# Score matmuls of batches 2 to 7 in two slots instead of four, and where their masks and v copies run

## Chip, cores and metric

One core of a Trainium2 chip. The metric is the device time of one execution in microseconds; the kernel before is quoted by the median of its runs.

## The reference

Two stages in a row. Attention over q, k, v of shape (8 batches, 8 heads, 576 positions, 64): the first four heads look at the last 32 positions (local mask), the other four at earlier positions with the same remainder by 32 (strided mask).

```python
mask_local = (rel >= 0) & (rel < stride)
mask_strided = (rel >= 0) & (pos[None, :] % stride == pos[:, None] % stride)
...
attn = exp(scores - max) ; attn /= sum
attn_out = attn @ v
```

Its output, as 4608 tokens of 512 features, goes through a two-layer network with w_in (512 x 2048), Mish and w_out (2048 x 512):

```python
h = x @ w_in
sp = np.where(h > 20.0, h, np.log1p(np.exp(np.minimum(h, 20.0))))
g = h * np.tanh(sp)
return (g @ w_out).astype(np.float32)
```

## The kernel before, in words

The network runs in nine blocks of 512 tokens, `t` = 0 to 8. Both its layers (`mlp1`, `mlp2_seven`) are built from seven products of half size with sums in front and behind, on TensorE (PE), VectorE (DVE) and ScalarE (ACT). The order of every engine's instructions is the order of the program; there is no scheduler.

The attention of batch `t + 1` is woven into the second layer of block `t`: `attn_steps` returns a list `at`, and after step `i` of the second layer the functions in `at[i]` are issued. A step is eight matmuls of `pso`; two steps are one product. This document calls block `t` the one with this `t`; blocks 1 to 6 hold batches 2 to 7 and follow the list that is changed here. Batch 1, in block 0, has another list that the diff leaves alone.

One batch's scores are in parts. Strided: `("s", 0)` and `("s", 1)` with 6 units of 72 columns, `("s", 2)` with 4. Local: `("l", 0)` and `("l", 1)` with 5 units of 96 columns, `("l", 2)` with 2. Each unit is two matmuls, one for each head of a pair, on the upper and lower 64 rows of the array (L310, tile `ps`). Steps:

- `Q` (`qk`, L294): score matmuls into an accumulator, then Exp on ACT (L318) into `P_s` or `P_l`.
- `M` and `G` (`mask`, L320, operation at L324): multiply by the 0/1 mask, on DVE (`M`) or on GpSimd (POOL, `G`).
- `V2` (`pv2`, L357): eight matmuls with v (L340, tile `po`), then reciprocal and normalization on DVE (L365, L366) into `x_s` or `x_l`.
- `X` (`xt`, L371): transposes of the result on PE (`trx`), copied to `xT` by ACT.

PSUM has eight banks: `acc0` and `acc1` of two banks each, two single banks `bank0`, `bank1` for the products of the second layer, and two single slots given out in turn by `tile_t` (`pt`). In the attention steps `x` is `acc0` and `y` is `acc1`. An accumulator can be written again when its last reader is done: `V2("s", 2, y)` waits until the normalization of `V2("s", 0, y)` has read `acc1`.

Around that, in the loop from L914: SP issues loads of local q, k, v and the transposes by DMA (`transpose_by_dma`, L205) that make `kTs`, `qTs`, `kTl`, `qTl`. POOL issues loads of strided q, k, v (`load_qk_str`, `load_early_v_str`), casts local v (`cast_v_loc`, two casts of 128x768) and local q and k, multiplies the local masks, and copies strided v from `vsr` to `vs` (`spread_v_str`). Ahead of the cast of local v POOL makes a small copy from `P_s[1]` to `held` (L943), whose only use is its wait: the cast does not begin before that strided mask is done.

Within the second layer each product ends in work for ACT or DVE: copies of `za` and `zc` out of PSUM, additions at L668, and sums of `gT` into `Sg` (L599), which later products read.

Of the kernel before, what the change touches and what calls it, by code (L numbers as in the profile page):

```python
# [12 lines left out]
AF = mybir.ActivationFunctionType  # L13
# [30 lines left out]
def kernel(ctx, tc, q, k, v, moe_w_in, moe_w_out, out):  # L44
    nc = tc.nc
# [61 lines left out]
    def acc(i, name):  # L107

        pool = ps_z[0] if i == 2 else ps_a
        return pool.tile([128, 2, 512], F32, tag=f"acc{i}", name=name)  # L110
# [10 lines left out]
    def tile_t(name):  # L121
        return ps_t.tile([128, 512], F32, tag="pt", name=name)
# [33 lines left out]
    def spread_v_str(b, eng):  # L156
        cast(eng, vs[b % 2][0:PN, :, :, 0:D], vs_raw().rearrange("p h (j d) -> p h j d", d=D))
# [119 lines left out]
    class Attn:  # L277
# [16 lines left out]
        def qk(self, parts, i_acc, ps=None):  # L294

            biased = ps is not None
            ps, o = ps if biased else acc(i_acc, "ps"), 0
            todo = []
            for kind, i in parts:
                w = WQ if kind == "l" else PN  # L300
                o0 = o
                for x, y in PARTS[kind][i]:
                    for e in range(2):
                        r = slice(64 * e, 64 * e + 64)
                        if kind == "l":
                            lhsT, rhs = kTl[r, y, WQ * x:WQ * x + 128], qTl[r, y, WQ * x:WQ * x + WQ]
                        else:
                            c0 = SU * (4 * y + x)
                            lhsT, rhs = kTs[r, c0:c0 + 128], qTs[r, c0:c0 + PN]
                        nc.tensor.matmul(  # L310
                            ps[:, e, o:o + w], lhsT=lhsT, rhs=rhs, start=not biased, stop=True,
                            skip_group_check=biased,
                        )
                    o += w
                todo.append((kind, i, o0, o - o0))
            for kind, i, o0, nw in todo:
                n, pt = (128, P_l[i]) if kind == "l" else (PN, P_s[i])
                nc.scalar.activation(pt[0:n, :, 0:nw], ps[0:n, :, o0:o0 + nw], AF.Exp, scale=scale)  # L318

        def mask(self, kind, i, meng):  # L320
# [77 lines left out]
    def attn_steps(b, x, y):  # L398

        a = Attn(b)  # L400
        Q = lambda i_acc, *parts: (lambda: a.qk(parts, i_acc))
        M = lambda kd, i: (lambda: a.mask(kd, i, nc.vector))
        V = lambda kd, i: (lambda: a.pv(kd, i))
        X = lambda kd, hf: (lambda: a.xt(kd, hf))
        s0, s1, sl2, l0, l1 = ("s", 0), ("s", 1), (("s", 2), ("l", 2)), ("l", 0), ("l", 1)
        if x == y:
            T = [(lambda n=n, eng=eng: t_step(b, *T_ORDER[n], eng)) for n, eng in enumerate(
                (None, None, None, None, None, nc.scalar, None, nc.scalar))]
            return [
                T[2:4], [Q(x, s0)],  # L410
                [M(*s0), Q(x, s1)],
                [lambda: spread_v_str(b, nc.vector), V("s", 0)],
                [V("s", 1), M(*s1), Q(x, ("s", 2))],
                [V("s", 2), T[4]],
                [V("s", 3), M("s", 2), T[5]],
                [V("s", 4), T[6]],
                [V("s", 5), T[7]],
                [V("s", 6), Q(x, l0)],
                [V("s", 7), M(*l0), Q(x, l1)],
                [X("s", 0), V("l", 0), M(*l1), Q(x, ("l", 2))],  # L420
                [X("s", 1), V("l", 1), M("l", 2)],
                [V("l", 2), V("l", 3)],
                [V("l", 4), V("l", 5)],
                [lambda hf=hf: a.xt("l", hf, nc.vector) for hf in range(2)],
            ], T[0:2]
        V2 = lambda kd, i, z: (lambda: a.pv2(kd, i, z))
        G = lambda kd, i: (lambda: a.mask(kd, i, nc.gpsimd))
        l2 = ("l", 2)
        at = [
            [],  # L430
            [Q(x, s0), Q(y, s1), M(*s0), M(*s1)],
            [],
            [V2("s", 0, y), Q(x, *sl2), M("s", 2)],
            [],
            [V2("s", 2, y), Q(x, l0), G(*l0)],
            [],
            [V2("s", 4, y), Q(x, l1), G(*l1), G(*l2), lambda: nc.scalar.preload_act_table(AF.Mish)],
            [],
            [V2("s", 6, y)],
            [V2("l", 0, x)],  # L440
            [X("s", 0), V2("l", 2, y), X("s", 1)],
            [V2("l", 4, x), X("l", 0)],
            [X("l", 1)],
        ]
        return at
# [10 lines left out]
    def mlp1(t, accs):  # L456
# [65 lines left out]
        def begin():  # L522
            z[1], z[3] = acc(accs[1], "psu"), acc(accs[0], "psu")
            z[2] = [bank(n, "psb")[:] for n in range(2)]
            z[5] = o_pool.tile([128, 2, DM], F32, tag="osb", name="p5")
            product(both(z[1]), 0, a11, b11, first=True)
            for n in range(2):
                nc.scalar.copy(z[2][n], z[1][:, n, :])
            sums_x(t, "2")
            product(both(z[3]), 0, s1, t1, first=True)  # L530
            sums_x(t, "3")
            if t == 1:
                sums_w_in()[3]()
            nc.scalar.copy(z[5][:], z[3][:])
            y[1] = tile_t("psv")[:]
            product([y[1]], 512, a11, b11, first=True)
# [265 lines left out]
    with tc.manual_schedule():  # L802
# [111 lines left out]
        for t in range(NBLK):  # L914
            if t == 0:
                x, y, z = accs
                at, ts = attn_steps(1, y, y)
                at[3] += [lambda: load_early_v_str(2), cast_v1]
                at[12].append(load_rest2)
                at[1].append(lambda: sums_w()[0](lo))  # L920
                at[7].append(lambda: sums_w()[0](hi))
                at[9].append(lambda: sums_w()[1](lo))
                at[11].append(lambda: sums_w()[1](hi))
                at[14].append(lambda: sums_x(1, "1"))
                at[15] += [
                    lambda: spread_v_str(2, Dv),
                ]
                out_accs = (z, x)
            else:
                if t == 1:  # L930
                    split_third()
                x, y = 0, 1
                gT, z, g1 = mlp1(t, (y, x) if t == 1 else (x, y))
                at = attn_steps(t + 1, x, y) if t + 1 < B else []
                if t == 1:
                    at[0].append(lambda: sums_w()[3](hi))
                if t + 2 < B:
                    at[10] += [lambda: transpose_by_dma(t + 2), lambda: load_v_loc(t + 2)]
                    if t + 3 < B:
                        at[10].append(lambda: load_early_v_str(t + 3))  # L940
                if t + 1 < B:
                    at[1] += [
                        lambda: Po.tensor_copy(held[:], P_s[1][0:1, 0, 0:4]),  # L943
                        lambda: cast_v_loc(t + 1, Po),
                    ]
                if t == 1:
                    at[1] += [lambda: load_qk_str(3), lambda: load_early_v_str(3)]
                if t < B - 3:
                    at[7 if t == 1 else 1].append(lambda: load_qk_str(t + 3))
                if t + 1 < B:  # L950
                    at[12].append(lambda: sums_x(t + 1, "1"))
            for i, g in enumerate(g1):
                g()
                if t == 0:
                    for s in ts if i == len(g1) - 1 else ():
                        s()
                    continue
            if t == 0:
                steps = mlp2(t, gT, out_accs, fc_major=True)
            elif t == NBLK - 1:  # L960
                mlp2_last(t, gT, z[5])
                break
            else:
                za, zc = [bank(i, "pso")[:].rearrange("p (n o) -> p n o", n=2) for i in range(2)]
                steps = mlp2_seven(t, gT, z[5], za, zc)
                if t + 1 == B:
                    steps[12] = lambda f=steps[12]: (sums_x(t + 1, "1"), f())
            for i, g in enumerate(steps):
                g()
                if i < len(at):  # L970
                    for s in at[i]:
                        s()
                if t > 0 and i == 9 and t + 2 < B:
                    cast_qk_loc(t + 2, Po, Po)
                    spread_v_str(t + 2, Po)
            if 0 < t < B - 3:
                load_qk_loc(t + 3)

# [29 lines left out]
```

## Time and profile before

| what | us |
|---|---|
| median of 3 runs | 291.82 (291.79 to 292.35) |
| the profiled execution's own time | 291.2 |
| its span | 289.4 |
| blocks 1 to 6, start to start (chain) | 29.7 each |
| PE busy in the span | 283.8 (98%) |
| DVE, ACT, POOL busy | 196.9, 192.8, 109.2 |

The profile is one execution. A row of the timeline gives the start from the span's begin, the length, the engine, the line, the operation and its tiles; rows of like instructions are merged and end in their number. What stands in square brackets is idle time of that engine before the row, and what ended it. Matmul ends are modelled, starts are recorded. The granted TensorE clock is 1.00 throughout.

### The profile page before, as it was taken

The numbers are of one execution on the slowest core, as the hardware profiler recorded it, in microseconds if no ns is written. First come the engines' busy times: TensorE is split into PE (matmuls) and PEld (weight loads), VectorE is DVE, ScalarE is ACT, GpSimd is POOL, SyncE is SP. The second block draws the span as 40 slices with busy tenths as digits, with TensorE's granted clock in tenths as the row PEclk, the third lists the DMA queues.
The fourth block names the chain that finished last, engine by engine and source line by source line (L and its number), as shares of the span: only waits on it lengthen the run. The fifth ranks groups of instructions, "written<-read, shape, count | busy, mean of one in ns | idle before, by whom it ended". The sixth has DMA issues, their size and how long they took to land.

```text
span 289.4 us, 7507 instructions
## 1 busy us (share of the span) xinstructions
PE 283.8 (98%) x3161; PEld 221.2 (76%) x3161; DVE 196.9 (68%) x398; ACT 192.8 (67%) x274; POOL 109.2 (38%) x122
## 2 busy tenths in 40 slices
PE   8999999999999999999999999999999999999994
PEld 3564455686898689868988888788977897788684
DVE  2273167899786777687777777777777767734742
ACT  1578643699657974898579757985799568507820
POOL 8375502140696059404960397027701710000000
PEclk9999999999999999999999999999999999999999
DMA  8999999999999999999999999999590030003004
GB/s 153 186 208 191 192 194 197 183 141 184 223 169 125 191 294 162 150 150 275 172 116 164 275 163 144 172 271 148 83 254 2 2 145 2 0 3 146 2 0 147
DMA packets 103742, 43.29 MB, mean 150 GB/s; under 512 B 86172, under 2 KB 99212, under 8 KB 103708
## 3 DMA queue, kind: packets, MB, share of 16 engines
q1 hardware_dynamic: 86620, 30.05, 61.8%
q0 software_dynamic: 16800, 12.51, 29.7%
q8 instruction: 25, 0.41, 0.6%
q10 hardware_dynamic: 288, 0.25, 0.3%
q14 instruction: 9, 0.07, 0.1%
HBM read 38.38 MB, written 9.44 MB: 165 GB/s over the span
## 4 chain that ended last, share of the span: by engine, by line
PE 95%; DVE 2%; ACT 2%; issue 0%; ACTq 0%
PE pso L691 30%; PE psu L503 10%; PE psh L472 10%; PE psv L503 8%; PE psb L503 7%; PE psb L472 5%; PE po L340 4%; PE pso L750 4%; PE ps L310 4%; PE pso L723 4%; PE un L264 3%; PE trx L379 2%; PE trx L389 1%; ACT Pl L318 1%; PE tr L236 1%; PE tr L250 1%
## 5 line engine op out<-in xcount | busy, mean ns | idle before, releaser
L691 PEld LDWEIGHTS <-gT 128*128 128x128 bf16 x448 | 41.8, 98 | 6.2
L503 PEld LDWEIGHTS <-w_in 128*128 128x128 bf16 x384 | 37.1, 98 | 8.4
L691 PE MATMUL pso<-w_out,gT 128*128 128x256 bf16 x336 | 41.0, 273 | 0.0
L691 PEld LDWEIGHTS <-Sg 128*128 128x128 bf16 x336 | 31.4, 98 | 4.7
L943 POOL COPY held<-Ps 1x4 bf16<-1x4 bf16 x6 | 3.5, 580 | 79.3 <-DVE Ps L324 79.3
L472 PEld LDWEIGHTS <-w_in 128*128 128x128 bf16 x208 | 20.2, 98 | 16.6 <-issue 0.5
L187 ACT COPY xT<-trx 128x576 bf16<-128x576 bf16 x30 | 18.4, 643 | 18.8 <-PE trx L389 13.3
L324 POOL TENSOR_TENSOR Pl<-Pl,consts_sb 128x960 bf16<-128x960 bf16 (+1 forms) x18 | 29.2, 1639 | 4.1 <-ACT Pl L318 3.5
L503 PEld LDWEIGHTS <-Sw 128*128 128x128 bf16 x288 | 28.2, 98 | 3.3
L472 PE MATMUL psh<-xT,w_in 128*128 128x512 bf16 (+1 forms) x136 | 29.4, 366 | 0.1
L691 PE MATMUL pso<-Tw,Sg 128*128 128x256 bf16 x224 | 26.7, 273 | 0.0
L318 ACT ACTIVATE Pl<-ps 128x960 bf16<-128x960 f32 (+1 forms) x24 | 19.3, 808 | 10.8 <-PE ps L310 10.8
L187 ACT COPY osb<-pso 128x512 f32<-128x512 f32 (+1 forms) x17 | 9.3, 549 | 21.9 <-PE pso L691 12.7
L512 ACT ACTIVATE gT<-psu 128x1024 bf16<-128x1024 f32 x16 | 16.4, 1024 | 8.4 <-PE psu L503 8.3
L318 ACT ACTIVATE Ps<-ps 72x864 bf16<-72x864 f32 (+1 forms) x24 | 18.6, 804 | 4.6 <-PE ps L310 4.6
L366 DVE TENSOR_TENSOR x_s<-po,rden 72x512 bf16<-72x512 f32 x28 | 19.2, 687 | 1.0
L599 DVE TENSOR_TENSOR psu<-psb,p 128x512 f32<-128x512 f32 x16 | 11.2, 698 | 11.8 <-PE psb L503 11.0
L483 ACT ACTIVATE gT<-psh 128x1024 bf16<-128x1024 f32 x16 | 16.2, 1024 | 4.3 <-PE psh L472 4.0
L324 DVE TENSOR_TENSOR Ps<-Ps,consts_sb 72x864 bf16<-72x864 bf16 (+1 forms) x21 | 15.1, 721 | 5.2 <-ACT Ps L318 5.2
L599 DVE TENSOR_TENSOR Sg<-gT 128x256 bf16<-128x256 bf16 (+2 forms) x32 | 12.8, 421 | 7.5 <-ACT gT L512 5.9
L503 PE MATMUL psu<-xT,w_in 128*128 128x256 bf16 x128 | 17.9, 272 | 0.0
L503 PE MATMUL psb<-Sx,w_in 128*128 128x256 bf16 x128 | 17.2, 272 | 0.0
(132 smaller groups left out, 607.0 us busy)
## 6 DMA issues: line engine op xcount, KB each, us to landing
vl<-in_v_dram SPq DMA_DIRECT2D x7, 768.0 KB, 6.3
out_dram<-osb SPq DMA_DIRECT2D x9, 512.0 KB, 5.3
out_dram<-p SPq DMA_DIRECT2D x7, 512.0 KB, 6.5
kl<-in_k_dram SPq DMA_DIRECT2D x6, 576.0 KB, 9.8
ql<-in_q_dram SPq DMA_DIRECT2D x6, 576.0 KB, 11.7
qs<-in_q_dram POOLq DMA_DIRECT2D x8, 288.0 KB, 10.7
vsr<-in_v_dram POOLq DMA_DIRECT2D x8, 288.0 KB, 8.0
w_in<-in_moe_w_in_dram POOLq DMA_DIRECT2D x4, 512.0 KB, 9.7
```

Source lines behind the costliest of these rows:

```text
L187: nc.scalar.copy(out_, in_)
L310: nc.tensor.matmul(ps[:, e, o:o + w], lhsT=lhsT, rhs=rhs, start=not biased, stop=True, skip_group_check=biased,)
L318: nc.scalar.activation(pt[0:n, :, 0:nw], ps[0:n, :, o0:o0 + nw], AF.Exp, scale=scale)
L324: meng.tensor_tensor(out=pm, in0=pm, in1=mk[0:n, :].unsqueeze(1).unsqueeze(1).to_broadcast([n, 2, nu, w]), op=ALU.mult,)
L340: nc.tensor.matmul(po[:, h, :], lhsT=pt[0:n, c0:c0 + 128], rhs=rhs, start=True, stop=True,)
L366: nc.vector.tensor_tensor(out=dst.rearrange("p e (h d) -> p e h d", h=4), in0=po[0:m, :, :, 0:D], in1=rden[0:m].unsqueeze(3).to_broadcast( ...
L472: nc.tensor.matmul(ps_u[:, o:o + n], lhsT=w_in[:, cc, fc * 128:(fc + 1) * 128], rhs=xT[:, cc, a:a + n], start=(cc == 2 and (o == 0 or len( ...
L483: nc.scalar.activation(to, tiles[g][:], AF.Mish)
L503: nc.tensor.matmul(p[:, 256 * j:256 * j + 256], lhsT=lhs[:, cc, f:f + 128], rhs=rhs[:, cc], start=(first and j == 0 and cc == 0), stop=(la ...
L512: nc.scalar.activation(gT[:, c:c + src.shape[1], 256 * half_t:256 * half_t + 256], src, AF.Mish,)
L599: nc.vector.tensor_tensor(out=out_, in0=in0, in1=in1, op=op)
L691: nc.tensor.matmul(ps[:, pair, :], lhsT=lhs(c, 128 * pair), rhs=rhs(c), start=(first and pair == 0 and c == 0), stop=(last and c == 7), sk ...
```

## The change

Four edits:

- In `attn_steps`, the third strided part and the third local part are scored at step 1 behind the first two strided parts, and the second local part at step 5 behind the first. The parts that come along write into the two single `pt` slots (`i_acc == "t"`), one for each head of the pair, so that each has two Exps, one for each slot, instead of one.
- The masks follow: `M("s", 2)` on DVE moves to step 1, `G(l2)` to step 3 and so ahead of the two other masks on POOL, `G(l1)` to step 5.
- `held` is copied from `P_s[2]` instead of `P_s[1]`: POOL's cast of local v comes behind the third strided mask.
- Strided v of batches 4 to 7 is spread by ACT at step 7 of blocks 2 to 5; that of batch 3 by DVE at the beginning of block 2, where the load of batch 4's follows. POOL spreads none of them any more.

```diff
         def qk(self, parts, i_acc, ps=None):
             biased = ps is not None
-            ps, o = ps if biased else acc(i_acc, "ps"), 0
+            o = 0
+            if i_acc == "t":
+                ps = None
+                by_e = [tile_t("ps") for _ in range(2)]
+            else:
+                ps = ps if biased else acc(i_acc, "ps")
+                by_e = [ps[:, e, :] for e in range(2)]
...
                         nc.tensor.matmul(
-                            ps[:, e, o:o + w], lhsT=lhsT, rhs=rhs, start=not biased, stop=True,
+                            by_e[e][:, o:o + w], lhsT=lhsT, rhs=rhs, start=not biased, stop=True,
...
                 n, pt = (128, P_l[i]) if kind == "l" else (PN, P_s[i])
+                if ps is None:
+                    for e in range(2):
+                        nc.scalar.activation(
+                            pt[0:n, e, 0:nw], by_e[e][0:n, o0:o0 + nw], AF.Exp, scale=scale
+                        )
+                    continue
...
         at = [
             [],
-            [Q(x, s0), Q(y, s1), M(*s0), M(*s1)],
+            [Q(x, s0), Q(y, s1), Q("t", *sl2), M(*s0), M(*s1), M("s", 2)],
             [],
-            [V2("s", 0, y), Q(x, *sl2), M("s", 2)],
+            [V2("s", 0, y), G(*l2)],
             [],
-            [V2("s", 2, y), Q(x, l0), G(*l0)],
+            [V2("s", 2, y), Q(x, l0), Q("t", l1), G(*l0), G(*l1)],
             [],
-            [V2("s", 4, y), Q(x, l1), G(*l1), G(*l2), lambda: nc.scalar.preload_act_table(AF.Mish)],
+            [V2("s", 4, y), lambda: nc.scalar.preload_act_table(AF.Mish)],
...
             sums_x(t, "3")
             if t == 1:
                 sums_w_in()[3]()
+            if t == 2:
+                spread_v_str(3, nc.vector)
+                load_early_v_str(4)
...
-                    if t + 3 < B:
+                    if t > 1 and t + 3 < B:
                         at[10].append(lambda: load_early_v_str(t + 3))
                 if t + 1 < B:
                     at[1] += [
-                        lambda: Po.tensor_copy(held[:], P_s[1][0:1, 0, 0:4]),
+                        lambda: Po.tensor_copy(held[:], P_s[2][0:1, 0, 0:4]),
                         lambda: cast_v_loc(t + 1, Po),
                     ]
...
+                if 1 < t < B - 2:
+                    at[7].append(lambda: spread_v_str(t + 2, Sc))
...
                     cast_qk_loc(t + 2, Po, Po)
-                    spread_v_str(t + 2, Po)
```

## The prediction

> **What bounds the kernel now.** I read the page first: busy shares, then the chain that ended last.
>
> ```profile
> PE 283.8 (98%) x3161; PEld 221.2 (76%) x3161; DVE 196.9 (68%) x398; ACT 192.8 (67%) x274; POOL 109.2 (38%) x122
> ...
> PE 95%; DVE 2%; ACT 2%; issue 0%; ACTq 0%
> ```
>
> TensorE (PE) is the chain, and in the list of waits it has two in all, 1.2 and 0.2 us, both in the first 17 us. So taking a wait away gains nothing; only less PE time does, and any new PE wait is paid in full. Next the timeline of block 5 (batch 6's attention between the products). Columns: start, us, engine, line, operation.
>
> ```profile
> 190.82 0.56 PE L310 MATMUL ps<-qTs,kTs 64*128 64x72 bf16 x24
> 191.32 1.92 PE L691 MATMUL pso<-Tw,Sg 128*128 128x256 bf16 x16
> 193.07 0.41 PE L340 MATMUL po<-vs,Ps 72*128 72x65 bf16 x8
> 193.41 0.30 PE L310 MATMUL ps<-qTs,kTs 64*128 64x72 bf16 x8
> 193.55 0.25 PE L310 MATMUL ps<-qTl,kTl 64*128 64x96 bf16 x4
> 193.74 1.92 PE L691 MATMUL pso<-Tw,Sg 128*128 128x256 bf16 x16
> 195.49 0.41 PE L340 MATMUL po<-vs,Ps 72*128 72x65 bf16 x8
> 195.83 0.39 PE L310 MATMUL ps<-qTl,kTl 64*128 64x96 bf16 x10
> 196.15 1.92 PE L691 MATMUL pso<-w_out,Sg 128*128 128x256 bf16 x16
> ...
> 200.32 0.41 PE L340 MATMUL po<-vs,Ps 72*128 72x65 bf16 x8
> 200.57 1.04 PE L691 MATMUL pso<-w_out,gT 128*128 128x256 bf16 x8
> ```
>
> Ends are modelled, so I use starts. Scores run as 64*128, all else on the full height. Eight po matmuls followed by a product take 0.25 us (200.32 to 200.57); followed by scores, 0.34 (193.07 to 193.41, 195.49 to 195.83): going into scores costs 0.09. Coming out: 24 narrow score matmuls take 0.50 us, the 8+4 take 0.33, the ten wide 0.32. With a time in proportion to columns this solves to 0.016 us for 72 columns plus a fixed 0.10 to 0.12. So a visit to scores costs about 0.19 us over its matmuls. This is PE time inside "busy", and each batch pays it four times.
>
> Then the engines that feed it in the same stretch, and GpSimd (POOL) in block 1, which is the same sequence 118.75 us earlier (first mask at 73.40 against 192.15).
>
> ```profile
> 191.23 1.66 ACT L318 ACTIVATE Ps<-ps 72x864 bf16<-72x864 f32 x2 [0.15 <-PE ps L310]
> ...
> 192.93 0.60 DVE L324 TENSOR_TENSOR Ps<-Ps,consts_sb 72x864 bf16<-72x864 bf16 x1 [0.18 <-ACT Ps L318]
> 193.46 0.68 DVE L599 TENSOR_TENSOR Sg<-gT,Sg 128x1024 bf16<-128x1024 bf16 x1
> 194.06 0.20 DVE L365 RECIPROCAL rden<-po 72x8 f32<-72x8 f32 x1
> 194.29 0.69 DVE L366 TENSOR_TENSOR x_s<-po,rden 72x512 bf16<-72x512 f32 x1
> 194.90 1.13 DVE L324 TENSOR_TENSOR Ps<-Ps,consts_sb 72x576 bf16<-72x576 bf16 x1
> ```
>
> ```profile
> 74.85 0.58 POOL L943 COPY held<-Ps 1x4 bf16<-1x4 bf16 x1 [12.44 <-DVE Ps L324]
> ...
> 79.36 4.84 POOL L324 TENSOR_TENSOR Pl<-Pl,consts_sb 128x960 bf16<-128x960 bf16 x3
> ...
> 84.09 0.43 PE L340 MATMUL po<-vl,Pl 128*128 128x65 bf16 x8
> ```
>
> The normalization of the first strided pair ends at 194.98 and frees acc1; PE wants it at 195.49, 0.51 spare. POOL starts only when the second strided mask is done, and its second wide mask ends at 83.33 (two of 2.01 us, starts 1.97 apart), 0.76 before PE reads it at 84.09.
>
> **Scores in two slots.** In blocks 1 to 6 the third strided part and local part 2 join the first visit; local part 1 joins local part 0. Four visits become two: 2 x 0.19 = 0.38 us, six times, 2.3 us. The matmuls themselves only move (0.22 us each lot). The two one-bank slots are free: their last readers, Mish of psv, end at 187.65, 3 us before. This is certain; what follows is what eats it.
>
> **The third mask goes ahead on VectorE (DVE).** It waits for its two half Exps. Exp of 864 columns takes 0.88 us, of 576 0.65: by that slope 0.41 for 288; starts lie 0.78 and 0.55 apart, so 0.31 for 288. The first Exp stays at 191.23, so the halves start at 192.80 and 193.11, end at 193.52. The mask starts 0.04 later as its neighbours do, 193.56, and takes 0.45 (445 ns is the shortest of its kind, in batch 1 where POOL is quiet): 194.00. The Sg subtraction behind it starts 0.08 before that end, 193.92, where it started at 193.46. From there to the end of the normalization the rows show 1.52 us: 195.44. PE starts 0.06 after such an end (15.49+0.69 to 16.24, its one such wait): 195.50. PE itself has saved one visit by then, 195.49-0.19 = 195.30. So it waits 0.20 us for acc1, in each of six blocks: 1.2 us. The second visit's saving, 0.19, comes behind that point and stays. Bounds: 0.05 to 0.35, from a mask that ends 0.15 earlier or later.
>
> [...]
>
> **POOL's masks.** The held copy now waits for the third mask: 194.00 against 193.53, so POOL's whole row is 0.47 later, and the small local mask (902 ns, 0.86 to the next start) goes first. Block 1, which has three DMA issues of 0.7 us in front: wide masks from 79.36+0.47+0.86 = 80.69, ending at 82.69 and 84.66. PE's first local pair, at 82.70 before, would come at 82.51 and waits to 82.75 (0.24); the next, due at 84.09-0.19+0.24 = 84.14, waits to 84.72 (0.58). Sum 0.82. Blocks 2 to 4 have two DMA issues: in block 3 the masks began at 137.95, so the second wide one ends at 143.25; due at 143.44-0.19 = 143.25, PE waits about 0.05. Blocks 5 and 6 have none: the mask ends near 201.3, wanted at 202.64, nothing.
>
> **The port.** The two casts of local v start 0.53 us after the held copy. Before, DVE's third mask met the second cast: it took 1.13 us, against 0.45 alone, in five of six blocks; in block 2 it took 0.60 and the cast pair 2.43 instead of 1.58. Now the gT subtraction stands there, at the same distance, since both chains hang on the end of one mask. As in the five it loses: it ends near 196.7, the second normalization near 197.6, PE needs it at 198.12; cost nothing. [...]
>
> **Edits that I cost at nothing.** The spread of v on ScalarE: not shown there; 2048 columns at 0.8 ns a column (0.88-0.65 over 288) plus 0.18 is 1.8 us, and the rows for it elsewhere are 0.69 (DVE) and 2.08 (POOL). It runs behind the table load, from about 199.3 to 201.1; ACT was idle 2.09 us until 203.03. An overshoot beyond 1.5 us would delay the xT copies and so the next block, four times. In block 2 DVE spreads v of batch 3, 0.69 us, into an idle of 0.97 before 90.54; 0.3 us is left; at 1.28 us (its contended instance) the psu sums behind it would start 0.3 late and PE's next psb products with them, once. The vsr loads are issued some 2 us earlier on POOL's queue, nothing waits for them soon. POOL loses five 2 us copies that PE never waited for. SP: in block 1 the ks load is issued 0.47 later, and the transposes queue behind it; the last, issued at 98.24, lands 3.0 us on, so at 101.7, and local part 2's scores now read it at 101.76+0.50+0.63 = 102.9 instead of 104.5. Spare 1.2. Next late after all this is acc1 for the strided pair at 200.1: its normalization ends at 199.9.
>
> **Sum.** Block 1: -0.38+0.20+0.82 = +0.64. Blocks 2 to 4: -0.38+0.20+0.05 = -0.13 each, -0.39. Blocks 5 and 6: -0.18 each, -0.36. Together -0.1 to -0.2 us. The profiled execution took 291.2 us (span 289.4), 0.6 below the median 291.82; the change is carried to the median: 291.65.
>
> **Rivals.** (1) The visits' gain comes through. If the third mask ends 0.2 us earlier than worked out, the acc1 wait is gone and POOL is 0.2 earlier: block 1 +0.44, blocks 2 to 4 -0.33 each, 5 and 6 -0.38 each: -1.3, 290.5. For: every PE row; against: ACT's and DVE's starts leave no such gap. (2) Slower: DVE wins the port from the second cast, as in block 2 before. The cast then waits about 0.6 us, and in blocks 1 to 4 nothing is left between POOL and PE, so each pays 0.6: two such blocks 292.85, all four 294.05. [...] (3) The scores of local part 2 in block 2 wait for their transposes, with DMA queues full: from 1.2 us of delay on; 1 us late gives 292.6. (4) The scores do not come to stand together: the new program's PE order shows them in one run, so no chance.
>
> **How the numbers follow.** About 0.2% (0.58 us) is what a measurement of this kernel can tell from no change. All waits hang on one instant, the end of the third mask; 0.1 us there moves six blocks, 0.6 us in sum. My case, within 0.1 of it, 0.42, own range 291.0 to 292.3; rival 1 0.32; rival 2 0.20; rival 3 and the like 0.06. That gives faster 0.33, same 0.41, slower 0.26. The range, 290.4 to 293.0, takes in rival 1 and two of rival 2's blocks.
>
> **What would show it.** Right: per block two runs of L316 scores, of 36 and 20 matmuls; a PE wait of about 0.2 us on x_s before the second strided pair; in block 1 PE waits on POOL's masks of 0.8 in sum; block 1 longer than 29.7 us, 5 and 6 shorter by 0.2; the third mask at 0.45. Wrong: no PE wait on x_s (rival 1), cast pairs of 2.2 us and up (rival 2), PE waits on qTl (rival 3), or gaps around scores that do not shrink.

## The result, and the profile after

| kernel | median us | executions | ratio to before, 95% interval |
|---|---|---|---|
| before, first comparison | 292.09 | 4 (291.79 to 292.57) | |
| changed, first comparison | 295.85 | 4 (294.29 to 299.15) | 1.0109 [1.0064, 1.0155] |
| changed again, c1 | 292.82 | 10 (291.62 to 295.77) | 1.0015 [0.9977, 1.0054] |
| changed again, c2 | 293.29 | 12 (291.35 to 298.89) | 0.9991 [0.9944, 1.0039] |
| changed again, c3 | 294.08 | 12 (291.44 to 300.13) | 0.9999 [0.9952, 1.0045] |

The first comparison says 1.1% slower. The forecast was 291.65 us with a range up to 293.0, and the measured 295.85 lies above it. The same program compared three times more is level with the kernel before, which itself ran from 290.88 to 299.14 us there. Ratios leave out executions more than 1.5% above the fastest of their kernel; medians and lists here leave out none.

The profiled execution of the changed kernel in the first comparison took 294.29 us (span 292.4, granted clock 1.00), 3.09 above the 291.2 of the profile before. The page's shares of the chain were 95% PE before; now:

```profile
PE 282.2 (96%) x3146; PEld 220.0 (75%) x3161; DVE 195.7 (67%) x399; ACT 200.2 (68%) x296; POOL 99.5 (34%) x117
...
PE 72%; DVE 6%; POOL 6%; DMA 6%; issue 3%; ACT 3%; SPq 2%; POOLq 0%; ACTq 0%; DVEq 0%
```

PE has 1.6 us less busy time (15 of its records are missing here, which is part of that) and the span is 3.0 longer: what grew is waiting. The list of PE's waits (engine, tile, line, releaser; us in total, times, longest) names it. Line numbers have moved by some lines: scores are L316, Exp L326 and L330, masks L336, `po` L352, normalization L378, sums L614, second layer's product L706, `held` L958.

```profile
PE po L352 <- POOL Pl L336: 1.8, 3, 1.2
...
PE ps L316 <- DMA qTl<-ql: 0.8, 1, 0.8
PE po L352 <- DVE x_s L378: 0.7, 2, 0.4
```

The timeline of block 5 answers to the one shown before; it lies 3 us later here.

```profile
193.71 0.69 PE L316 MATMUL ps<-qTs,kTs 64*128 64x72 bf16 x32
194.24 0.25 PE L316 MATMUL ps<-qTl,kTl 64*128 64x96 bf16 x4
194.42 1.92 PE L706 MATMUL pso<-Tw,Sg 128*128 128x256 bf16 x16
196.18 0.41 PE L352 MATMUL po<-vs,Ps 72*128 72x65 bf16 x8
196.42 1.91 PE L706 MATMUL pso<-Tw,Sg 128*128 128x256 bf16 x16
198.43 0.42 PE L352 MATMUL po<-vs,Ps 72*128 72x65 bf16 x8
198.79 0.60 PE L316 MATMUL ps<-qTl,kTl 64*128 64x96 bf16 x20
199.32 1.92 PE L706 MATMUL pso<-w_out,Sg 128*128 128x256 bf16 x16
201.68 0.42 PE L352 MATMUL po<-vs,Ps 72*128 72x65 bf16 x8 [0.45 <-DVE x_s L378]
```

Scores now stand in two runs, of 36 and 20. Read the starts: a product of 16 matmuls is followed by `po` after 1.76 us where nothing waits (194.42 to 196.18; before 1.75). The second takes 2.01 (196.42 to 198.43), a wait of 0.25 for `acc1`. The third takes 2.36 (199.32 to 201.68), a wait of 0.60 that was not forecast. ACT, DVE and POOL in the same stretch:

```profile
194.12 1.66 ACT L330 ACTIVATE Ps<-ps 72x864 bf16<-72x864 f32 x2 [0.16 <-PE ps L316]
195.68 0.70 ACT L326 ACTIVATE Ps<-ps 72x288 bf16<-72x288 f32 x2
```

```profile
195.82 1.12 DVE L336 TENSOR_TENSOR Ps<-Ps,consts_sb 72x864 bf16<-72x864 bf16 x2 [0.17 <-ACT Ps L330]
196.86 0.68 DVE L614 TENSOR_TENSOR Sg<-gT,Sg 128x1024 bf16<-128x1024 bf16 x1
...
197.69 0.69 DVE L378 TENSOR_TENSOR x_s<-po,rden 72x512 bf16<-72x512 f32 x1
198.30 2.49 DVE L614 TENSOR_TENSOR gT<-gT 128x1024 bf16<-128x1024 bf16 x1
200.72 0.19 DVE L377 RECIPROCAL rden<-po 72x8 f32<-72x8 f32 x1
200.94 0.69 DVE L378 TENSOR_TENSOR x_s<-po,rden 72x512 bf16<-72x512 f32 x1
```

```profile
197.54 1.58 POOL L189 CAST vl<-vl 128x768 bf16<-128x768 f32 x2
199.06 0.30 POOL L225 MEMSET vl<- 32x256 bf16 x1
199.34 5.27 POOL L336 TENSOR_TENSOR Pl<-Pl,consts_sb 128x384 bf16<-128x384 bf16 x3
```

The gT sum takes 2.49 us instead of 0.68: from 198.30, when POOL's second cast is starting, through that cast and through the small mask behind it (902 ns from 199.34). The normalization that `acc1` hangs on comes after it in DVE's order.

Where the 3.1 us lie is read best by the distance from one block's first `psu` product to the next (the chain of waits lists them):

| block | before | changed, first profile | changed, c1 |
|---|---|---|---|
| 1 | 29.70 | 30.25 | 30.25 |
| 2 | 29.68 | 32.02 | 29.55 |
| 3 | 29.68 | 29.53 | 29.54 |
| 4 | 29.72 | 29.86 | 29.87 |
| 5 | 29.67 | 30.15 | 30.15 |
| 6 | 29.68 | 29.53 | 29.53 |

Five blocks repeat within 0.01 us between the two executions, and differ from before by the same amounts. Block 2 does not repeat. So there are two parts: a steady one, +0.55, -0.13, -0.14, +0.15, +0.48, -0.15, in sum +0.76 us by c1, whose profiled execution took 292.0 us; and 2.47 us more in block 2 of the first profile. There, PE:

```profile
102.83 0.21 PE L316 MATMUL ps<-qTl,kTl 64*128 64x96 bf16 x2
103.80 0.22 PE L316 MATMUL ps<-qTl,kTl 64*128 64x96 bf16 x2 [0.76 <-DMA qTl<-ql]
...
114.77 0.43 PE L352 MATMUL po<-vl,Pl 128*128 128x65 bf16 x8 [1.17 <-POOL Pl L336]
...
116.72 0.37 PE L352 MATMUL po<-vl,Pl 128*128 128x65 bf16 x6 [0.32 <-POOL Pl L336]
```

and POOL, first in this profile and then the same rows in c1:

```profile
108.62 1.59 POOL L189 CAST vl<-vl 128x768 bf16<-128x768 f32 x2 [2.46 <-DMA vl<-in_v_dram]
...
111.83 4.83 POOL L336 TENSOR_TENSOR Pl<-Pl,consts_sb 128x384 bf16<-128x384 bf16 x3
```

```profile
106.15 1.58 POOL L189 CAST vl<-vl 128x768 bf16<-128x768 f32 x2
...
109.36 4.85 POOL L336 TENSOR_TENSOR Pl<-Pl,consts_sb 128x384 bf16<-128x384 bf16 x3
```

The last transpose of batch 3's local q landed at 103.76 us (101.28 before), and local v at 108.57 (105.24 before). The first held PE, the second held POOL's cast, hence its masks, hence PE. In c1 both were in time and PE waited for neither.

### The profile page after: what moved, and what is told of

It is laid out like the page before. It is cut to its first block, busy times and chain, and to the rows that moved or that the text cites. A ratio compares the mean times of both kernels' runs of the same rounds, so it can differ in the third digit from the quotient of the medians.

```text
span 292.4 us, 7529 instructions
## 1 busy us (share of the span) xinstructions
PE 282.2 (96%) x3146; PEld 220.0 (75%) x3161; DVE 195.7 (67%) x399; ACT 200.2 (68%) x296; POOL 99.5 (34%) x117
## 4 chain that ended last, share of the span: by engine, by line
PE 72%; DVE 6%; POOL 6%; DMA 6%; issue 3%; ACT 3%; SPq 2%; POOLq 0%; ACTq 0%; DVEq 0%
PE pso L706 15%; PE psu L515 10%; PE psh L484 9%; PE psv L515 8%; PE psb L515 7%; PE pso L765 4%; POOL Pl L336 4%; PE psb L484 4%; PE pso L738 4%; DMA ql<-in_q_dram 3%; PE un L264 3%; PE po L352 3%; DMA vl<-in_v_dram 2%; ACT Ps L330 2%; PE ps L316 2%
## 5 line engine op out<-in xcount | busy, mean ns | idle before, releaser
L706 PEld LDWEIGHTS <-gT 128*128 128x128 bf16 x448 | 41.8, 98 | 5.8
L706 PE MATMUL pso<-w_out,gT 128*128 128x256 bf16 x336 | 41.0, 273 | 0.0
L958 POOL COPY held<-Ps 1x4 bf16<-1x4 bf16 x6 | 3.5, 580 | 93.9 <-DVE Ps L336 93.9
L706 PEld LDWEIGHTS <-Sg 128*128 128x128 bf16 x336 | 31.5, 98 | 4.3
L336 POOL TENSOR_TENSOR Pl<-Pl,consts_sb 128x960 bf16<-128x960 bf16 (+1 forms) x18 | 29.6, 1670 | 0.2
L706 PE MATMUL pso<-Tw,Sg 128*128 128x256 bf16 x224 | 26.7, 273 | 0.0
L614 DVE TENSOR_TENSOR psu<-psb,p 128x512 f32<-128x512 f32 x16 | 11.2, 699 | 14.7 <-PE psb L515 13.8
L378 DVE TENSOR_TENSOR x_s<-po,rden 72x512 bf16<-72x512 f32 x28 | 19.2, 686 | 1.0
L330 ACT ACTIVATE Ps<-ps 72x864 bf16<-72x864 f32 (+1 forms) x18 | 14.7, 856 | 4.6 <-PE ps L316 4.6
L614 DVE TENSOR_TENSOR Sg<-gT 128x256 bf16<-128x256 bf16 (+2 forms) x32 | 12.8, 421 | 7.1 <-ACT gT L524 5.6
L484 PE MATMUL psb<-xT,w_in 128*128 128x512 bf16 (+1 forms) x72 | 16.4, 355 | 0.0
L738 PE MATMUL pso<-w_out,gT 128*128 128x512 bf16 x59 | 15.8, 380 | 0.5 <-issue 0.3
```

What stands on the lines that cost most here:

```text
L336: meng.tensor_tensor(out=pm, in0=pm, in1=mk[0:n, :].unsqueeze(1).unsqueeze(1).to_broadcast([n, 2, nu, w]), op=ALU.mult,)
L378: nc.vector.tensor_tensor(out=dst.rearrange("p e (h d) -> p e h d", h=4), in0=po[0:m, :, :, 0:D], in1=rden[0:m].unsqueeze(3).to_broadcast( ...
L484: nc.tensor.matmul(ps_u[:, o:o + n], lhsT=w_in[:, cc, fc * 128:(fc + 1) * 128], rhs=xT[:, cc, a:a + n], start=(cc == 2 and (o == 0 or len( ...
L614: nc.vector.tensor_tensor(out=out_, in0=in0, in1=in1, op=op)
L706: nc.tensor.matmul(ps[:, pair, :], lhsT=lhs(c, 128 * pair), rhs=rhs(c), start=(first and pair == 0 and c == 0), stop=(last and c == 7), sk ...
L738: nc.tensor.matmul(p[:, ot % 2, :], lhsT=gT[:, fc, 128 * ot:128 * ot + 128], rhs=w_out[:, fc, :], start=(fc == 0), stop=(fc == 15),)
```

## The experiments

Each kernel is the changed one with the edit shown, unless said otherwise. Block times are given in the order 1 to 6.

**The changed kernel again (c1, c2, c3).** No edit.

> The changed kernel as it is, beside its variants. Theory A: block 2 loses most, in PE waits on qTl and, through the late landing of local v, on GpSimd's masks; about 1.2% over before. Theory B (what is lost is the waits for acc1 and GpSimd in every block, and block 2's landings were chance): block 2 near the others here, total within 1 us of before.

> The changed kernel again, beside the next three. Theory D (in every execution: 0.38 us saved in each of six blocks, 0.27 lost to acc1, 0.8, 0.3 and 0.6 lost to GpSimd and the port in blocks 1, 4 and 5; on top, in some executions, block 2 waits for transposes and local v that land late): 291.5 to 292.5 where they land in time, up to 4 us more where not.

> The changed kernel a third time. Theory D (a steady part near zero, plus late landings in blocks 1 and 2 in some executions): level with before within 0.4%, 291.4 to 292.6 in the executions without late landings. If the first comparison's 1.1% is the kernel's own: 295 us.

Times stand in the first table. The steady blocks came out as in the first profile each time, within 0.07 us (c3: 30.24, 29.58, 29.55, 29.87, 30.16, 29.53). In c2 block 2 took 30.61, for another reason: the load of `vsr` that DVE's spread at the start of block 2 reads landed at 92.06 us, and the sums behind it came late.

```profile
92.09 0.69 DVE L189 COPY vs<-vsr 72x2048 bf16<-72x2048 bf16 x1 [1.37 <-DMA vsr<-in_v_dram]
```

```profile
93.44 0.60 PE L515 MATMUL psb<-Sx,w_in 128*128 128x256 bf16 x4 [0.62 <-DVE psu L614]
```

So block 2 has three ways to be late, each in some executions only: transposes, local v, and `vsr`. Further runs repeat the +0.76 of the steady part, and not the 1.1%.

**Two slots alone (e1).** Masks, `held`, spreads and the `vsr` loads as before. Of the edit, the lines on the masks:

```diff
-            [Q(x, s0), Q(y, s1), Q("t", *sl2), M(*s0), M(*s1), M("s", 2)],
+            [Q(x, s0), Q(y, s1), Q("t", *sl2), M(*s0), M(*s1)],
...
-            [V2("s", 0, y), G(*l2)],
+            [V2("s", 0, y), M("s", 2)],
...
-            [V2("s", 2, y), Q(x, l0), Q("t", l1), G(*l0), G(*l1)],
+            [V2("s", 2, y), Q(x, l0), Q("t", l1), G(*l0)],
...
-            [V2("s", 4, y), lambda: nc.scalar.preload_act_table(AF.Mish)],
+            [V2("s", 4, y), G(*l1), G(*l2), lambda: nc.scalar.preload_act_table(AF.Mish)],
```

> Scores in two slots alone: masks at their old steps (third strided mask at step 3, local masks 0, 1, 2 in the old order), held copied from P_s[1], v spread by GpSimd as before. Theory A (the loss is GpSimd's later row, and what it does to the loads of block 1 and so to the transposes and local v of block 2): the visits' 0.38 us in each of six blocks is kept, GpSimd's row and the loads stand as before, about 289.8 us. Theory B (the loss comes from the moved spreads and vsr loads): also about 289.8. Theory C (the loss comes from scoring local part 2 so early, its transposes being late): PE still waits some 1 us for qTl in block 2, 290.8 or more.

Median 292.35 of 10 (289.32 to 300.75), ratio 0.9956 [0.9906, 1.0007]. Blocks 29.35, 33.35, 29.65, 29.38, 30.56, 29.25. Block 6 shows the saving whole, 0.43 us. Block 2 was late on transposes and local v. Block 5 lost because POOL's copy of strided v, which the kernel before has too, here meets DVE's first sum of block 5 (2.53 us instead of 0.41), and PE waits 1.2 us for it.

**Only `held` back (e2).**

```diff
-                        lambda: Po.tensor_copy(held[:], P_s[2][0:1, 0, 0:4]),
+                        lambda: Po.tensor_copy(held[:], P_s[1][0:1, 0, 0:4]),
```

> The changed kernel with one thing undone: held is copied from P_s[1], so GpSimd may begin the cast of local v 0.47 us earlier, beside the third strided mask. Theory A: GpSimd's row in block 1 and the loads behind it are up to 0.4 us earlier, block 2's qTl wait shrinks, 293 to 294 us, unless the cast and VectorE's mask and sums block each other, which gives the 0.4 us back. Theory B and C: as the changed kernel, 294.3 to 296.2, or worse by the collisions.

Median 291.69 of 10 (291.16 to 299.56), ratio 0.9938 [0.99, 0.9976]. Blocks 30.22, 29.46, 29.47, 29.80, 30.08, 29.46: each 0.03 to 0.09 less than in c1, with the extra of blocks 1, 4 and 5 all still there. In sum they are still 0.36 us longer than before, so the ratio under 1 does not come from these blocks; the executions of before beside it ran from 290.91 to 297.67. Taking `held` from the earlier mask brought little, because the copy now runs beside the third mask and takes 1.02 us instead of 0.58, so that POOL's casts came only 0.03 to 0.08 us earlier in each block than in c1:

```profile
74.64 1.02 POOL L958 COPY held<-Ps 1x4 bf16<-1x4 bf16 x1 [12.07 <-DVE Ps L336]
75.62 1.58 POOL L189 CAST vl<-vl 128x768 bf16<-128x768 f32 x2
```

**The spreads back on POOL (e3), and the spreads alone moved (e4, the kernel before with only that part).** The edit of e3, whose reverse on the kernel before is e4:

```diff
-            if t == 2:
-                spread_v_str(3, nc.vector)
-                load_early_v_str(4)
...
-                    if t > 1 and t + 3 < B:
+                    if t + 3 < B:
...
-                if 1 < t < B - 2:
-                    at[7].append(lambda: spread_v_str(t + 2, Sc))
...
+                    spread_v_str(t + 2, Po)
```

> The changed kernel with GpSimd spreading strided v and loading vsr as before. Theory A: the spreads are not what costs: 294 to 296 us as changed. Theory B: block 2's late landings go away, 291.5 to 292 us. Theory C: as changed.

> The kernel before with only the spreads moved (ScalarE in blocks 2 to 5, VectorE and the vsr load at the beginning of block 2). Theory A and C: 291.8 us as before, within 0.3. Theory B: slower by 1 us or more, with transposes and local v of block 2 landing late.

e3: median 297.94 of 10 (294.48 to 303.2), ratio 1.0135 [1.0086, 1.0185]. Blocks 30.24, 30.84, 29.53, 29.85, 31.41, 29.53. Block 5 has 1.26 more than in c1: POOL's copy runs when DVE wants to sum, and PE waits for the sum. The profiled execution took 294.48, the shortest of the ten; what the others lost beyond that was not profiled.

```profile
177.42 2.49 DVE L611 TENSOR_TENSOR Sx<-xT 128x512 bf16<-128x512 bf16 x1
```

```profile
177.75 1.89 POOL L189 COPY vs<-vsr 72x2048 bf16<-72x2048 bf16 x1
```

```profile
179.96 1.05 PE L515 MATMUL psu<-Sx,Sw 128*128 128x256 bf16 x8 [1.15 <-DVE Sx L611]
```

e4: median 293.94 of 10 (291.1 to 296.95), ratio 0.9977 [0.9926, 1.0029], all blocks as before (29.67 to 29.72). So ScalarE spreads for nothing in the steady blocks, as forecast. With the two slots, POOL's copy cost about 1.3 us in block 5 of both profiles that kept it, with the masks as before (e1) and with the changed ones (e3), so the move pays there.

**The masks and `held` as before, the two slots and the new spreads kept (e7).**

```diff
-            [Q(x, s0), Q(y, s1), Q("t", *sl2), M(*s0), M(*s1), M("s", 2)],
+            [Q(x, s0), Q(y, s1), Q("t", *sl2), M(*s0), M(*s1)],
...
-            [V2("s", 0, y), G(*l2)],
+            [V2("s", 0, y), M("s", 2)],
...
-            [V2("s", 4, y), lambda: nc.scalar.preload_act_table(AF.Mish)],
+            [V2("s", 4, y), G(*l2), lambda: nc.scalar.preload_act_table(AF.Mish)],
...
-                        lambda: Po.tensor_copy(held[:], P_s[2][0:1, 0, 0:4]),
+                        lambda: Po.tensor_copy(held[:], P_s[1][0:1, 0, 0:4]),
```

> As the one with masks and held back, but block 1's loads where they were. Theory A: GpSimd's row as in the kernel before; 289.5 if ks and qs land as before, more where block 2's transposes come late by chance of the queues: 289.5 to 292. Theory B: 289.5.

Blocks 29.24, 29.71, 29.25, 29.30, 29.26, 29.25: every block but the second saves 0.41 to 0.46, the two visits without a new wait; in the second, POOL's cast waited half a us for local v. Four executions, median 292.66: 288.77, 289.76 (the profiled one), 295.57 and 298.0; too few for an interval. In the steady blocks the masks' new places and the later `held` thus cost 0.76 + 6 x 0.43 = 3.3 us, and turn the gain of the two slots into a loss.

**The small local mask last instead of first (e11).**

```diff
-            [V2("s", 0, y), G(*l2)],
+            [V2("s", 0, y)],
...
-            [V2("s", 2, y), Q(x, l0), Q("t", l1), G(*l0), G(*l1)],
+            [V2("s", 2, y), Q(x, l0), Q("t", l1), G(*l0), G(*l1), G(*l2)],
```

> The changed kernel with one thing: GpSimd's small local mask last, as before, instead of first. Theory D: the wide masks end 0.86 us earlier, so PE's waits on GpSimd in block 1 (0.8) and 4 (0.3) go, and in block 5 GpSimd pauses before the first wide mask, lets VectorE's sum in and the 0.6 us wait goes: 1.5 to 1.7 us under the changed kernel.

Median 292.47 of 12 (289.84 to 298.77), ratio 0.9954 [0.9909, 0.9998]. Blocks 29.47, 30.70, 29.53, 29.57, 29.53, 29.53: the extras of blocks 1, 4 and 5 are gone with this one line, as expected; block 2 lost to the late `vsr` again. In block 5 the gT sum now takes 1.37 us, since the wide mask that comes first has to wait for its Exp and leaves a pause:

```profile
195.74 1.37 DVE L614 TENSOR_TENSOR gT<-gT 128x1024 bf16<-128x1024 bf16 x1
```

```profile
196.50 0.30 POOL L225 MEMSET vl<- 32x256 bf16 x1
197.71 4.84 POOL L336 TENSOR_TENSOR Pl<-Pl,consts_sb 128x960 bf16<-128x960 bf16 x3 [0.90 <-ACT Pl L330]
```

**Local part 2's early reading (e8, e9).** e8 scores it at step 3; e9 is the kernel before with part 2 scored at step 1 in the slots, and four visits kept.

```diff
-            [Q(x, s0), Q(y, s1), Q("t", *sl2), M(*s0), M(*s1), M("s", 2)],
+            [Q(x, s0), Q(y, s1), Q("t", ("s", 2)), M(*s0), M(*s1), M("s", 2)],
...
-            [V2("s", 0, y), G(*l2)],
+            [V2("s", 0, y), Q(x, l2), G(*l2)],
```

> The changed kernel with local part 2 scored at step 3 again: three visits instead of two, 0.19 us more in a block, of which the wait for acc1 gives back the same; so with transposes in time as the changed kernel within 0.2 us. Theory D: qTl is read 2.2 us later, so PE does not wait for it, and the upper end of the times comes down by 1 us; late local v stays. If qTl was no cause: the same times as the changed kernel throughout.

> The kernel before with one thing: local part 2 is scored at step 1 into the two slots, still four visits, masks and spreads as before. Theory D: as before where the transposes land in time (291.8), with PE waits on qTl of about 1 us in block 2 where not; median 0 to 1 us over before. If reading qTl early is harmless: as before throughout.

e8: median 294.35 of 12 (291.58 to 300.15), ratio 0.9997 [0.9951, 1.0043]; its profile had the strided transposes late by 1.40 us at PE, so it says nothing on the local ones. The wait for `acc1` was gone, the 2.49 us sum was there in blocks 5 and 6. e9: median 292.41 of 12 (291.31 to 300.87), 0.9981 [0.9948, 1.0014]; the last transpose landed at 102.36 and PE did not wait for it. Its block 2 took 30.27, 0.59 more than before, for another reason: `vsr` landed at 91.64 instead of 89.80, and POOL's copy from it then met a DVE sum (1.95 us instead of 0.41). The other blocks are as before, so reading early costs nothing when the transposes are in time. Whether it makes executions worse when they are not was not isolated.

**Loads earlier or in another order (e5, e6, e14, e12).** e5 issues block 1's strided loads at the beginning of the block; e6 adds to it the masks and `held` of e7. e14 issues them between `held` and the cast. e12 moves DVE's spread of block 2, and the load behind it, after a later sum of the same block.

```diff
# e5
+                if t == 1:
+                    load_qk_str(3)
+                    load_early_v_str(3)
...
-                if t == 1:
-                    at[1] += [lambda: load_qk_str(3), lambda: load_early_v_str(3)]
# e14
-                        lambda: cast_v_loc(t + 1, Po),
...
+                if t + 1 < B:
+                    at[1].append(lambda: cast_v_loc(t + 1, Po))
# e12
-            if t == 2:
-                spread_v_str(3, nc.vector)
-                load_early_v_str(4)
...
+            if t == 2:
+                spread_v_str(3, nc.vector)
+                load_early_v_str(4)
```

> The changed kernel, but block 1's loads of strided k, q and v are issued at the beginning of block 1, while GpSimd idles, and no longer between the cast of local v and the masks. Theory A: GpSimd's row in block 1 is 2.1 us shorter, its two waits there (0.8 us) go, ks and qs land some 10 us earlier, and block 2's waits on qTl and local v go: 291 to 292 us. Theory B: only block 1's 0.8 us goes, about 294.

> Early loads, and the masks and held as in the kernel before (third strided mask at step 3, local masks in the order 0, 1, 2, held from P_s[1]); two slots and ScalarE's spreads kept. Theory A and B: no wait for acc1, none on GpSimd; 0.38 us in each of six blocks remains, 289.5 us, faster than both kernels.

> The changed kernel with block 1's three loads issued ahead of the cast of local v instead of behind it, GpSimd's row otherwise the same. Theory D: ks, qs and vsr are issued 1.8 us earlier, the transposes and local v of block 2 land 1 to 2 us earlier, block 2's waits shrink; block 1's 0.8 us on GpSimd stays: 291 to 292. If the landings are set by the amount in flight rather than by the issue: no change.

> The changed kernel with VectorE's spread of batch 3's v (and the vsr load behind it) some 8 us later in block 2, behind the sums of gT. Theory D: where vsr lands late, the changed kernel's VectorE stands still in front of the psu sums and PE waits up to 1.1 us; here none of that: up to 1 us less, and nothing where vsr lands in time.

e5: median 298.26 of 4 (294.61 to 299.5), ratio 1.0153 [1.0075, 1.023], a miss: now batch 2's transposes, which these loads run beside, were late in block 1, and batch 3's in block 2; PE waited for both.

```profile
PE ps L316 <- DMA qTl<-ql: 4.5, 2, 2.7
```

e6: 293.27 of 10 (290.84 to 296.88), 1.0018 [0.9981, 1.0055], with 1.58 us of that wait in block 1 and blocks 3 to 6 at 29.25 to 29.29; it is not faster than before, as it was expected to be. e14: 295.98 of 12 (291.59 to 298.57), 1.0025 [0.9971, 1.0079]; in its profile (291.59) transposes and local v landed 1.5 and 2.0 us earlier than before and nothing of block 2 waited, but the times fell into two heaps. e12: 294.87 of 12 (292.56 to 296.52), 1.0074 [1.0034, 1.0114], a miss: its profile has no wait for `vsr`, but the last transpose landed at 105.2.

```profile
105.25 0.22 PE L316 MATMUL ps<-qTl,kTl 64*128 64x96 bf16 x2 [2.01 <-DMA qTl<-ql]
```

In the profiles of e5, e6 and e12, with loads moved, PE waited 4.5, 1.4 and 2.0 us for late transposes of local q; in that of e14 it waited for none.

**Towards a faster version (e13, e15, e16).** e15 is e7 with e14's order of loads; e13 has e12's edit as well; e16 is e15 with local part 2 scored at step 3.

> Two slots and ScalarE's spreads, with masks and held as in the kernel before, VectorE's spread later and block 1's loads ahead of the cast. Theory D: the steady part is 0.38 us in each of six blocks, 289.3 to 289.6 us without late landings, and fewer of those: faster than both kernels by 0.8%.

> Two slots and the moved spreads kept; masks, their order and held as in the kernel before; block 1's loads ahead of the cast. Theory D: no steady wait, 0.38 us saved in each of six blocks: 288.7 to 289.5 us where nothing lands late, 1 to 4 us more where qTl does; ratio to before 0.99.

> The same with local part 2 scored at step 3, so three visits. Theory D: 0.19 us saved in each of six blocks, 290.0 to 290.6 where nothing lands late, and fewer executions above 292 than the one with two visits.

| kernel | median us | executions | ratio to before, 95% interval | blocks 1, 3 to 6 | block 2 |
|---|---|---|---|---|---|
| e13 | 293.12 | 12 (288.69 to 297.15) | 0.9946 [0.9889, 1.0004] | 29.25 to 29.29 | 33.97 |
| e15 | 293.84 | 6 (288.61 to 295.06) | 0.9851 [0.9773, 0.9928] | 29.25 to 29.30 | 35.96 |
| e16 | 295.86 | 6 (294.59 to 297.52) | 1.011 [1.0053, 1.0166] | 29.46 to 29.51 | 33.66 |

e15's ratio rests on its two executions at 288.6; the other four took 293.15 to 295.06, and the kernel before beside it had a median of 293.69, so by medians it is no gain. The profile of e15 took 295.06: by its starts PE lost 2.37 us in block 2 to strided transposes that landed at 104.58, and 1.54 to local ones. The lowest times of e7, e13 and e15 are 288.77, 288.69 and 288.61, which is 2.73, 2.19 and 2.52 below the lowest of before beside them (291.5, 290.88, 291.13), near the 6 x 0.43 = 2.6 us of the visits. So a version that beats both kernels exists where nothing is late, but most executions do not reach it; in the two profiles of e13 and e15 it was late landings that took the gain away. Of the forecasts the floor of e13 and e15 came true (288.6 to 289.8); "faster than both kernels" for e13 and "fewer executions above 292" for e16 did not. e16 gives back one visit (0.21 us a block) and was late all the same.

## Why the prediction was wrong

Two kinds of step failed. In all four profiles of the changed kernel, "cost nothing" for VectorE's gT sum in block 5 (PE lost 0.60 us to it, and the block came out 0.66 over its forecast) and the one row taken for the DMA issues of blocks 2 to 4 (0.28 in block 4). In the first comparison, "Spare 1.2" in front of the local transposes of block 2, and local v, which the sum leaves out: together 2.47 us in the one profile. The first kind alone stays inside the range; the second carried the time out of it. Why the transfers came late stays open, and so does the 1.6 us by which the median, 295.85, lies over the profiled execution.

**Saved visits: right.** Forecast 0.38 us a block, measured 0.43 (e7, 29.68 to 29.25). Scores stand in runs of 36 and 20. ("All else on the full height" misreads the rows: `po` with `vs` runs as 72*128. The price of a visit was taken from starts, and does not rest on it.)

**Third mask and `acc1`: right.** The mask took 0.45 as forecast. The Sg subtraction behind it starts 17.58 us after block 5's start (196.86 less 179.28), where 17.53 was worked out (193.92 less 176.39), and PE waited 0.25 instead of 0.20. Rival 1, no such wait, is refuted.

**The two half Exps: right.** They took 0.40 and 0.41 us, started 0.29 apart, and ended 2.26 us after the start of the first Exp (196.38 less 194.12), where 2.29 was worked out from the rows' starts (193.52 less 191.23).

**POOL in block 1: right.** Forecast 0.24 + 0.58 = 0.82; PE's starts give 0.29 + 0.49 = 0.78, and the block came out at +0.55 against +0.64. In blocks 2 (when in time), 3 and 6, forecast -0.13, -0.13 and -0.18, the measured are -0.13, -0.14 and -0.15.

**POOL in block 4: wrong by 0.28.** "Blocks 2 to 4 have two DMA issues", it says, and takes block 3's row for all three. In block 4 POOL pauses between its two issues (for what, the profile does not show), so that its masks begin 0.3 later in the block; c1 has it, and so has the profile before, where nothing waited for it:

```profile
167.23 0.72 POOL L126 DMA_DIRECT2D qs<-in_q_dram  x1 [0.27 <-issue]
167.96 4.96 POOL L324 TENSOR_TENSOR Pl<-Pl,consts_sb 128x960 bf16<-128x960 bf16 x3
```

That is 21.29 us after block 4's start (146.67), against 20.95 in block 3 (137.95 less 117.00). The forecast had PE waiting 0.05 for POOL already, with nothing left between them; 0.34 more goes almost whole to PE.

**VectorE's sum beside POOL in block 5: wrong by 0.66, the largest step of the steady part.** "It ends near 196.7, the second normalization near 197.6, PE needs it at 198.12; cost nothing." The sum did lose to the second cast, as forecast, and took 1.36 to 1.37 us in blocks 1 to 4 and 6 of c1. In block 5 it took 2.49 to 2.50 in every profile of the changed kernel: behind the cast come only a small memset and then the small mask, which the change itself had put there, and the sum ended 0.55 us behind the end of that one (200.79 against 200.24 in the first profile), as in block 1 it ended 0.55 behind the end of the cast (77.92 against 77.37). PE lost 0.60 in the product behind it. The forecast looked at who wins one meeting, and not at what POOL has queued next. e11 shows it: with the wide mask first, and so a pause, 1.37. Block 6 has the same rows on POOL as block 5 and took 1.36, while the small mask took 1.10 instead of 0.90, so there it was POOL's that got longer; in e8 the sum of block 6 took 2.49 as well. Why it gets in between at one time and not at another stays open. With the masks of e7 the sum takes 0.68 in all six blocks. Rival 2, DVE ahead of the cast, was not seen in any of c1's blocks, and neither was a cast 0.6 us longer. What the prediction calls the port is in no run as such: the rows show by how much an instruction of one engine gets longer beside one of the other.

In block 5 of the first profile the sum starts at 198.30 and the second cast at 198.3, a tie, and it is the sum that got longer (2.49 us; the cast took its 0.82). In the profile before, the third mask and the second cast of block 5 start together at 194.9 too, and there also it was DVE's that got longer (1.13 instead of 0.45; the cast 0.82).

**Sum of the steady part.** -0.1 to -0.2 was forecast, +0.76 measured; 0.28 and 0.66 less 0.07 elsewhere make the 0.87 between. That alone gives 291.82 + 0.76 = 292.6, inside the range and, as a ratio of 1.0026, within the intervals of c1 to c3.

**Rival 3: right in kind, too small in chance.** It had a chance of 0.06 on a spare of 1.2 us. In the first profile the last transpose was issued 1.3 later than before (99.52 against 98.24) and landed 2.5 later, and PE lost 0.93 by its starts (102.83 to 103.80, less two matmuls); local v, which the forecast did not cost at all, came 3.3 later and cost PE another 1.33 + 0.48. The profile before had a sign of it: in block 2 POOL's cast, behind `held`, already waited for local v.

```profile
105.29 2.43 POOL L189 CAST vl<-vl 128x768 bf16<-128x768 f32 x2 [0.18 <-DMA vl<-in_v_dram]
```

A spare of 1.2 us was judged from one landing time of one execution. The landing times of one kind of transfer in this stretch range over 9 us: strided q's transposes were issued at 86.7 to 90.2 us in all profiles, and landed between 95.3 and 104.6. The DVE spread in block 2 had a spare of 0.3, and was late in c2, e11 and e15.

**Open.** What decides when the transfers of blocks 1 and 2 land; hence why the four executions of the first comparison all had such a loss, if they did (one was profiled), and most later ones of the same program did not. Chance may have had a part: there no execution of before was above 295 us and three of four changed ones were; later it was 31 of 131 of before and 13 of 34 changed, too few to tell these shares apart. The later comparisons ran on five chips, each beside its own executions of before; what part the chip has was not tested. That the early loads and the early read make late landings more frequent was not shown: e2, which differs from the changed kernel in one operand, had its last transpose at 100.48.

One regularity stands in the 20 profiles. In six (c1, c2, c3, e2, e4, e11) strided k of batch 3 landed so late that its transposes were issued behind POOL's loads of batch 4's strided k and q. There the last transpose landed at 100.1 to 101.9 us, and PE waited for none. In the other fourteen they were issued ahead of the second of these loads, the last transpose landed at 99.7 to 107.9, and in eight of them PE waited in block 2. Starting the transposes later thus went with earlier landings. No run held them back on purpose, so this is not shown as the cause.

## What to carry to other kernels

When an engine that had slack is put a few tenths from the critical one, take its row from every repetition of the loop and not from one: a pause that cost nothing before (here 0.27 us in one block of six) is then paid in full. Where an instruction gets longer beside another engine's (here DVE's sum beside POOL's cast, 1.36 us instead of 0.68), count what that engine has queued behind it (2.49 with the mask), not only the instruction that it meets. And a spare of 1 us in front of a DMA read from one execution is no spare: where landing times range as they do here, over 9 us, look at the landing times of several executions before putting a reader earlier.

## What the runs showed of the hardware

A DVE subtraction on 128x1024 bf16, 0.68 us alone (e7), took 1.36 beside one POOL cast of 0.82 us (block 1 of the first profile), and 2.49 (block 5) where POOL went on with a mask of 0.90 us 0.22 after the cast, though by its record the subtraction (198.30) had started before that mask (199.34). POOL lost less: its three masks took 5.27 us there instead of 4.84 in block 4.

In e15, after PE had stood still for most of 102 to 105 us, the granted clock fell for the stretch that follows (windows view: stretch, its length, busy time of PE, PEld, DVE, ACT, POOL, then PEclk, DMA share and GB/s):

```profile
102.00:105.00 3.00, 0.69 (x22) 0.43 (x22) 0.69 (x1) 0.59 (x1) 0.00 (x0) 1.00 1.25 122
107.40:110.70 3.30, 3.30 (x24) 2.49 (x23) 0.72 (x3) 1.34 (x5) 0.58 (x1) 0.51 1.10 234
```

PE was busy through all of that stretch; at the full clock its work would have taken 1.68 us (3.30 x 0.51), an estimate that puts 1.62 on the clock. The late transfers of e15 thus cost PE more than the waits themselves: of the 6.7 us that its block 2 has over a block in time (35.96 less 29.25), PE's starts give 3.9 to the waits for transposes, 1.1 to sums behind the late `vsr`, and 1.65 to the slow stretch. In e5 the granted clock was 0.78 from 106 to 110 us, where PE was idle for 1.8 us, and 0.80 from 110 to 114; the mean clock of e13's profile is 0.994, as is that of e15's. But in e5 PE was also idle for 2.7 us between 72 and 76, and the clock was 1.00 there and up to 80; and e12, with a wait of 2.0, has a mean clock of 0.999. So no length of pause can be given. One stretch lowers the mean clock of an execution to 0.994 (e15). The changed execution of 299.15 us in the first comparison has 0.989, which by that estimate is about two of them, so it probably stood still as well.
